# Layer norm's 1e-5 on GpSimd, a new order of all operations, and another turn of the w2 buffers (gated long convolution and token mixer, one core)

## The chip, the core and the metric

The kernel runs on one core of a Trainium2 chip. Five engines of that core work from queues of their own, each strictly in order: TensorE (PE in the profile, its weight loads PEld), VectorE (DVE), ScalarE (ACT), GpSimd (POOL) and SyncE (SP), which issues most DMAs. An instruction waits in its queue until the semaphores it needs have their values, and all behind it on that engine wait with it. The metric is the device time of one execution in microseconds, as a median of several runs.

## The reference, cut to what matters

```python
x = A_q                                            # 1 x 2048 x 640, bfloat16
g = sigmoid((x * gate_w).sum(-1, keepdims=True))
# a: a long convolution
k_shift = sum over t of k_pad[:, t:t+S] * shift_k[:, 3-t]     # 4 taps
kv = k_shift * v
y  = irfft(rfft(kv, 4096) * rfft(ssm_k, 4096))[:2048]         # along the sequence, per channel
a  = x * (y + kv * ssm_D)
# b: a token mixer
h = (x - mean) / sqrt(var + 1e-5)                  # layer norm over the 640 channels
u = gelu(einsum("bsd,sf->bdf", h, w1) + b1)        # w1: 2048 x 1536
b = transpose(einsum("bdf,fs->bds", u, w2) + b2)   # w2: 1536 x 2048
return g * a + (1 - g) * b
```

## The kernel before, in words

The sequence is cut into 16 tiles of 128 rows and four blocks of 512. **Branch a** is done as matrices: ssm_k is transposed on TensorE and brought into frequencies (stages wt and wf, `w_turn`, L1025, and `w_freq`, L1064, with the tables TFs, TFc and TS), joined and summed on VectorE (`w_comb`, L1098, `w_sums`, L1108). The blocks of k and v are loaded (`kv_load` and `kv_block`, L1124 to L1172): kT by a transposing DMA, four taps as small matmuls against the diagonal matrices dg, the result turned back by a second transposing DMA into kt, then products and sums on VectorE into v and es, and frequencies on TensorE (`a_freq`, stage af, L1174). `pair` (L1204) multiplies block spectra A with filter spectra W into Z on VectorE; `inverse` (L1272) brings Z back. **Branch b** is the layer norm (L915 to L945) with h for every tile, `mlp1` (stage m1, L961; h times w1, gelu to gT) and `mlp2` (stage m2, L1235; gT times w2). The `epilogue` (L1320) gates and adds, four tiles at a time; the last block goes tile by tile, the very last tile (`fin`) straight from PSUM in two halves.

**Layer norm.** Nine groups, two of one tile and seven of two. For each: `bn_stats` and `bn_aggr` on VectorE (L931, L933), then the addition of 1e-5 to the variance, vpe (L935; the instruction itself is in the helper `ts`, L664), then vpe to the power −0.5 on GpSimd, rstd (L936). Then, for tiles marked D, h on VectorE (L940, through L665); for the others a small product nmr on VectorE and h on ScalarE (L944, L945, through L695).

**w2.** `w2_load(q)` (L1228) brings 256 columns of w2 (768 KB, eight pieces) into one of three buffers, w2_0 to w2_2; `mlp2(q)` uses the same map. A load into a buffer waits for the last matmul that read it. In the profile all three show as `w<-in_B_w_dram`.

**What sets the order.** Every operation is first recorded with its engine (`_Plan.add`) and gets a number, 863 in all, in the order in which the program names it. `ORDER` (L433) is a hand-kept list of those 863 numbers; `_Plan.run` (L399) emits the operations in that order, so each engine's queue has its own operations in the order of the list, and gives matmul groups the free one of four PSUM slots that was used longest ago. `_Tracker` (L18) sets the semaphore waits. The planner's `cost` of an operation is kept with it but isn't used when a list is replayed.

Helpers that give most lines of the profile: matmuls L311; `tt` L657; `ts` L664 and L665; copies L672; fills L675; `act` L695; gathers L726; scatters L732; plain DMAs L262 and L265, transposing ones L260. SP's queue has all plain and transposing DMAs; GpSimd's has the gathers of reversed rows of v (`kv_load`), the scatters, and the DMAs that add into the output.

Of the kernel before, what the change touches and what calls it, by code (L numbers as in the profile page):

```python
# [12 lines left out]
ALU = mybir.AluOpType  # L13
# [409 lines left out]
def _checked(items, offs, base, top):  # L423
# [7 lines left out]


ORDER = [  # L433
# [36 lines left out]
]  # L470


def _build(nc, A_q, A_k, A_v, A_shift_k, A_ssm_k, A_ssm_D, B_x, B_w1, B_b1, B_w2, B_b2, gate_w, out):
# [19 lines left out]
    with ExitStack() as es:  # L493
# [146 lines left out]
        def bc(ap, dims):  # L640
            return bass.AP(tensor=ap.tensor, offset=ap.offset, ap=dims)
# [129 lines left out]
        def dram(t, off, ap):  # L771
            return bass.AP(tensor=t.tensor, offset=t.offset + off, ap=ap)

        b = bufs
# [107 lines left out]
        def rows(t, t0, cnt, w, c0, cw, step=1):  # L882
            return dram(t, t0 * 128 * w + c0, [[w, 128], [step * 128 * w, cnt], [1, cw]])
# [34 lines left out]
        for gi, (t0, cnt) in enumerate(groups):  # L918
            pr = 1.0 + t0 * 0.08
            plan.tag = f"ln{t0}"  # L920
            dma(x[:, t0:t0 + cnt, :], rows(A_q, t0, cnt, D, 0, D), f"x{gi}", pr)
            for t in range(t0, t0 + cnt):
                if LMODE[t] == "A":
                    act(h[:, t, :], x[:, t, :], ACT.Copy, pr, scale=-1.0 / (D * sq), acc=b["mv"][:, t, 0:1])
                    act(h[:, t, :], x[:, t, :], ACT.Square, pr, scale=1.0 / sq, bias=b["mv"][:, t, 0:1],
                        acc=b["mv"][:, t, 1:2])
                    continue
                for c in range(2):
                    o_ = b["stats"][:, t, c * 6:(c + 1) * 6]
                    i_ = x[:, t, c * HD:(c + 1) * HD]  # L930
                    vop("DVE", 0.393, (lambda o_, i_: lambda e: e.bn_stats(o_, i_))(o_, i_), [i_], [o_], pr, kind="bn")  # L931
                o_, i_ = b["mv"][:, t, :], b["stats"][:, t, :]
                vop("DVE", 0.11, (lambda o_, i_: lambda e: e.bn_aggr(o_, i_))(o_, i_), [i_], [o_], pr, kind="ba")  # L933
            sl = slice(t0, t0 + cnt)
            ts(b["vpe"][:, sl], b["mv"][:, sl, 1], 1e-5, None, ALU.add, None, pr, cost=0.07)  # L935
            vop("POOL", 0.7, (lambda o_, i_, e_: lambda e: e.tensor_tensor(o_, i_, e_, ALU.pow))(  # L936
                b["rstd"][:, sl], b["vpe"][:, sl], bc(c_mh, [[8, 128], [0, cnt]])), [b["vpe"][:, sl], c_mh], [b["rstd"][:, sl]], pr, kind="pow")
            for t in range(t0, t0 + cnt):
                if LMODE[t] == "D":
                    ts(h[:, t, :], x[:, t, :], b["mv"][:, t, 0:1], b["rstd"][:, t:t + 1],  # L940
                       ALU.subtract, ALU.mult, pr + 0.1, cost=0.36)
                else:
                    o_, a_, r_ = b["nmr"][:, t:t + 1], b["mv"][:, t, 0:1], b["rstd"][:, t:t + 1]
                    ts(o_, a_, r_, sq if LMODE[t] == "A" else -1.0, ALU.mult, ALU.mult, pr, cost=0.07)  # L944
                    act(h[:, t, :], x[:, t, :], ACT.Identity, pr, bias=o_, scale=r_)  # L945
# [280 lines left out]
                    tt(Z[:, 2, f0:f1, :], Z[:, 2, f0:f1, :], Z[:, 0, f0:f1, :], ALU.add, pr)  # L1226

        def w2_load(q):  # L1228
            nm = f"w2_{(0, 1, 0, 1, 2, 0, 1, 2)[q]}"
            dma(b[nm][:, :, :], dram(B_w2, q * 256, [[S, 128], [128 * S, FT], [1, 256]]), nm, 40.0 + q)  # L1230

        ost = []
# [2 lines left out]
        def mlp2(q):  # L1235
            plan.tag = f"m2_{q}"
            w2_load(q)
            w2 = b[f"w2_{(0, 1, 0, 1, 2, 0, 1, 2)[q]}"]
            o_ = b[f"o{(q // 2) % NO}"]
            turned = q >= 6  # L1240
            w2r = b[f"w2r{q % 2}"]
# [228 lines left out]
```

## Time and profile before

| | |
|---|---|
| median of 3 runs | 187.47 us (187.36 to 187.61) |
| profiled execution | 188.28 us |
| its span, first to last event | 186.4 us |
| granted TensorE clock | 1.00 |
| TensorE busy | 176.8 us |
| VectorE busy | 178.8 us |
| ScalarE busy | 127.1 us |
| GpSimd busy | 35.3 us |
| read from and written to HBM | 26.03 and 7.54 MB |

Times in the profile count from the start of the span. Busy time of an engine is the union of its instructions, which overlap where they are pipelined: a matmul of 0.30 us is followed by the next after about 0.14. A row of a timeline gives the start, the length of a run of like instructions, engine, line, output and inputs, and in brackets how long the engine sat idle before it and what it waited for. A row of a group gives the count, then after the bar the busy time in us, the mean of one in ns, and after the second bar the idle time ahead of them. DMA issues show on SPq.

### The profile page before, as it was taken

Reading aid. Unit: us, or ns where it says so; the run is one execution under the profiler, and the core shown is the slowest. Engines: PE = TensorE matmul, PEld = TensorE weight load, DVE = VectorE, ACT = ScalarE, POOL = GpSimd, SP = SyncE. Lnnn points to the kernel's source line nnn. Section 1 sums busy time; section 2 is a strip of 40 time slices with the busy share of each in tenths; the row PEclk is TensorE's granted clock in tenths of the full one; section 3 lists DMA queues with packets and bytes.
Section 4 is the critical chain, followed back from the end, with each engine's and each line's share of the span. In section 5 each row is a group of like instructions: output and inputs, shape, how many; then the busy total and the mean of one; then the engine's idle time right before and its main releaser. Section 6 shows DMA issues by size and latency. Waiting matters only on the chain.

```text
span 186.4 us, 3923 instructions
## 1 busy us (share of the span) xinstructions
PE 176.8 (95%) x1578; PEld 122.0 (65%) x1578; DVE 178.8 (96%) x252; ACT 127.1 (68%) x205; POOL 35.3 (19%) x68
## 2 busy tenths in 40 slices
PE   7778899999999999999999999999999999999992
PEld 2255667566667766777777777677776777777771
DVE  7999999999999999999899999999999999999784
ACT  3979899879499579638830146644889555875870
POOL 8367067610000000011000000000000500350262
PEclk9999999999999999999999999999999999999999
DMA  5999999798995998598769999988999998999394
GB/s 148 344 311 242 168 184 232 212 212 211 240 333 120 221 234 195 117 224 219 161 143 175 270 252 211 216 156 263 282 270 294 281 190 242 320 182 234 72 136 146
DMA packets 80448, 40.37 MB, mean 217 GB/s; under 512 B 39400, under 2 KB 80238, under 8 KB 80430
## 3 DMA queue, kind: packets, MB, share of 16 engines
q1 hardware_dynamic: 77694, 37.18, 80.9%
q0 software_dynamic: 2736, 2.95, 10.2%
q8 instruction: 12, 0.20, 0.5%
q14 instruction: 6, 0.05, 0.1%
HBM read 26.03 MB, written 7.54 MB: 180 GB/s over the span
## 4 chain that ended last, share of the span: by engine, by line
PE 64%; DVE 23%; DMA 6%; issue 2%; POOL 2%; ACT 1%; DVEq 0%; POOLq 0%
PE pp L311 64%; DVE stats L931 6%; DMA w<-in_B_w_dram 6%; DVE v L657 3%; DVE en L657 3%; DVE es L657 2%; DVE idx L664 2%; DVE W L657 2%; POOL rstd L936 1%; DVE h L665 1%; DVE eo L1023 1%; DVE mv L933 1%; DVE A L657 1%; DVE xe L657 1%; DVE dg L1012 1%
## 5 line engine op out<-in xcount | busy, mean ns | idle before, releaser
L311 PE MATMUL pp<-h,w 128*128 128x320 bf16 x384 | 56.6, 299 | 0.2
L311 PE MATMUL pp<-gT,w 128*128 128x320 bf16 x336 | 48.7, 299 | 0.6 <-DMA w<-in_B_w_dram 0.5
L311 PEld LDWEIGHTS pp<-h,w 128*128 128x128 bf16 x384 | 36.8, 98 | 15.9 <-issue 1.6
L311 PEld LDWEIGHTS pp<-gT,w 128*128 128x128 bf16 x336 | 32.5, 98 | 13.9 <-DMA w<-in_B_w_dram 1.1
L657 DVE TENSOR_TENSOR tt<-A,W 128x3840 bf16<-128x3840 bf16 (+2 forms) x16 | 27.8, 1738 | 0.2
L695 ACT ACTIVATE A<-pp 128x640 bf16<-128x640 f32 x32 | 21.3, 703 | 8.1 <-PE pp L311 8.1
L657 DVE TENSOR_TENSOR Z<-Z,tt 128x3840 bf16<-128x3840 bf16 (+1 forms) x14 | 26.1, 1867 | 0.1
L262 POOL DMA_DIRECT2D out_dram<-xe x3 | 4.1, 1367 | 66.4 <-DVE y L657 57.5
L695 ACT ACTIVATE pq<-pp 128x640 bf16<-128x640 f32 x16 | 11.0, 703 | 7.2 <-PE pp L311 7.1
L695 ACT ACTIVATE gT<-pp,bf 128x640 bf16<-128x640 f32 x12 | 9.5, 791 | 7.9 <-PE pp L311 7.9
L695 ACT ACTIVATE o<-pp,c,omg 128x640 bf16<-128x640 f32 x13 | 11.5, 881 | 4.6 <-PE pp L311 4.6
L931 DVE BATCH_NORM_STATS2 stats<-x 128x6 f32<-128x320 bf16 x32 | 13.7, 473 | 0.0
L695 ACT ACTIVATE xe<-xe,gg 128x640 bf16<-128x640 bf16 x16 | 12.8, 827 | 0.9 <-DMA xe<-rows_q 0.8
L695 ACT ACTIVATE ks<-pp 128x512 bf16<-128x512 f32 (+1 forms) x24 | 11.3, 523 | 3.1 <-PE pp L311 3.1
L657 DVE TENSOR_TENSOR Z<-A,W 128x3840 bf16<-128x3840 bf16 x6 | 12.8, 2153 | 0.5 <-PE pp L311 0.5
L695 ACT ACTIVATE W<-pp 128x640 bf16<-128x640 f32 x18 | 12.1, 720 | 1.5 <-PE pp L311 1.5
L675 POOL MEMSET W<- 1x640 bf16 x4 | 2.7, 665 | 51.1 <-ACT nq L695 49.8
L657 DVE TENSOR_TENSOR W<-W 128x2560 bf16<-128x2560 bf16 x8 | 11.9, 1486 | 0.2
L311 PE MATMUL pp<-kT,dg 64*64 64x256 bf16 x320 | 10.2, 270 | 0.3 <-ACT Wo L695 0.3
L657 DVE TENSOR_TENSOR Z<-Z 128x1280 bf16<-128x1280 bf16 (+1 forms) x16 | 10.0, 653 | 0.1
L311 PE MATMUL pp<-eo,TFc 128*128 128x320 bf16 x48 | 8.9, 300 | 1.2 <-ACT TFc L695 1.2
L262 POOL DMA_DIRECT2D out_dram<-rows_o x6 | 7.0, 1355 | 15.3 <-DMA out_dram<-o 13.2
(156 smaller groups left out, 305.1 us busy)
## 6 DMA issues: line engine op xcount, KB each, us to landing
w<-in_B_w_dram SPq DMA_DIRECT2D x24, 256.0 KB, 4.5
w<-in_B_w_dram SPq DMA_DIRECT2D x8, 768.0 KB, 6.2
wnat<-in_A_ssm_k_dram SPq DMA_DIRECT2D x4, 640.0 KB, 5.2
x<-in_A_q_dram SPq DMA_DIRECT2D x7, 320.0 KB, 6.5
out_dram<-o SPq DMA_DIRECT2D x6, 320.0 KB, 5.4
v<-in_A_v_dram SPq DMA_DIRECT2D x4, 320.0 KB, 3.9
rows_q<-in_A_q_dram SPq DMA_DIRECT2D x8, 160.0 KB, 3.5
xe<-rows_q SPq DMA_DIRECT2D x8, 160.0 KB, 6.1
```

The costliest lines, as they stand in the source:

```text
L262: ins = engobj.dma_start(out_ap, in_ap, accum_op=ALU.add)
L311: ins = self.nc.tensor.matmul(ps_ap, lhsT=lhsT, rhs=rhs, start=start, stop=stop)
L657: return vop(eng, c, lambda e: e.tensor_tensor(out_, in0, in1, op), [in0, in1], [out_], pr, kind="tt")
L664: return e.tensor_scalar(out_, in0, s1, None, op0=op0)
L665: return e.tensor_scalar(out_, in0, s1, s2, op0=op0, op1=op1)
L675: return vop(eng, 0.03 + nel(ap) / 1200.0, lambda e: e.memset(ap, val), [], [ap], pr, kind="ms")
L695: return e.activation(out_, src, func, **kw)
L931: vop("DVE", 0.393, (lambda o_, i_: lambda e: e.bn_stats(o_, i_))(o_, i_), [i_], [o_], pr, kind="bn")
L933: vop("DVE", 0.11, (lambda o_, i_: lambda e: e.bn_aggr(o_, i_))(o_, i_), [i_], [o_], pr, kind="ba")
L936: vop("POOL", 0.7, (lambda o_, i_, e_: lambda e: e.tensor_tensor(o_, i_, e_, ALU.pow))(b["rstd"][:, sl], b["vpe"][:, sl], bc(c_mh, [[8, 12 ...
L1012: vop("DVE", 1.45, lambda e: e.tensor_tensor(o_, ib, sb, ALU.mult), [i_, s_ap], [o_], 1.8, kind="tt")
L1023: vop("DVE", 0.74, lambda e: e.tensor_copy(dst, src()), [src], [dst], 0.3, ps=[p_], kind="ev")
```

## The change

Three edits.

1. The addition of 1e-5 (nine of them, the vpe operations) goes from VectorE to GpSimd, with another planner cost.
2. `ORDER` is another list of the same 863 numbers. Its first operations keep their places up to the exchange of a neighbour here and there; from about the 48th on, nearly every place differs. On GpSimd an addition stands ahead of its power, mostly right ahead; the powers no longer stand together, and the first gather for v0 (number 291), which stood behind the fill of a TFs row (number 41), stands ahead of it. The products and sums of TensorE, VectorE and ScalarE are the same, and so are the DMAs.
3. The pieces of w2 go to buffers 0, 1, 0, 2, 1, 0, 2, 1 in place of 0, 1, 0, 1, 2, 0, 1, 2: pieces 3 and 6 to buffer 2, pieces 4 and 7 to buffer 1.

```diff
 ORDER = [
-    0, 3, 7, 10, 62, 1, 2, 5, 9, 8, 244, 13, 11, 243, 14, 31, 206, 12, 19, 137, 26, 4, 15, 21,
-    126, 6, 54, 27, 33, 22, 91, 32, 16, 23, 63, 153, 64, 20, 211, 24, 287, 65, 17, 209, 103, 34, 25, 37,
...
-    825, 826, 832, 792, 831, 783, 793, 796, 781, 835, 780, 836, 797, 794, 803, 845, 855, 841, 784, 856, 804, 842, 857, 844,
-    840, 852, 805, 782, 853, 846, 798, 806, 799, 854, 800, 858, 860, 801, 861, 802, 859, 847, 862, 848, 850, 849, 851,
+    0, 3, 7, 10, 62, 1, 2, 5, 9, 8, 244, 13, 11, 243, 14, 31, 12, 206, 19, 137, 26, 4, 15, 21,
+    126, 6, 54, 27, 33, 91, 22, 32, 16, 23, 153, 63, 64, 20, 211, 24, 287, 65, 17, 209, 103, 34, 25, 66,
...
+    829, 834, 791, 833, 792, 781, 835, 783, 836, 797, 780, 803, 844, 841, 856, 845, 793, 840, 782, 842, 804, 843, 846, 805,
+    860, 794, 784, 847, 861, 798, 855, 806, 862, 852, 799, 853, 800, 857, 801, 854, 858, 802, 848, 859, 850, 849, 851,
 ]
...
             sl = slice(t0, t0 + cnt)
-            ts(b["vpe"][:, sl], b["mv"][:, sl, 1], 1e-5, None, ALU.add, None, pr, cost=0.07)
+            ts(b["vpe"][:, sl], b["mv"][:, sl, 1], 1e-5, None, ALU.add, None, pr, eng="POOL", cost=0.25)
             vop("POOL", 0.7, (lambda o_, i_, e_: lambda e: e.tensor_tensor(o_, i_, e_, ALU.pow))(
...
         def w2_load(q):
-            nm = f"w2_{(0, 1, 0, 1, 2, 0, 1, 2)[q]}"
+            nm = f"w2_{(0, 1, 0, 2, 1, 0, 2, 1)[q]}"
...
-            w2 = b[f"w2_{(0, 1, 0, 1, 2, 0, 1, 2)[q]}"]
+            w2 = b[f"w2_{(0, 1, 0, 2, 1, 0, 2, 1)[q]}"]
```

Numbers that matter at the end: 848 and 850 are the two halves of the last tile on VectorE, 860 and 861 additions of o, 847 the operation that adds the bias c2 to the last tile; 798 to 802 are TensorE's last groups. At the start of the w1 matmuls 163 is TensorE's first; 197 is a group of w1 matmuls that stands as the 75th operation of TensorE in both lists.

64 rows, old and new, of the table ORDER are left out of this document.

## The prediction

> **What bounds the kernel now.** I read the page's busy line first, then the chain of work that ended last, then the busy time in stretches.
>
> ```profile
> PE 176.8 (95%) x1578; PEld 122.0 (65%) x1578; DVE 178.8 (96%) x252; ACT 127.1 (68%) x205; POOL 35.3 (19%) x68
> PE 64%; DVE 23%; DMA 6%; issue 2%; POOL 2%; ACT 1%; DVEq 0%; POOLq 0%
> 49.76 67.37 PE pp L311 x644
> 117.26 15.95 PE pp L311 x151
> 133.21 10.31 DMA w<-in_B_w_dram
> 143.57 36.61 PE pp L311 x268
> 180.20 0.89 ACT o L695
> 183.14 0.55 DVE xe L1358
> 8.00:20.00 12.00, 9.46 (x86) 6.19 (x86) 12.00 (x39) 10.44 (x19) 6.58 (x8) 1.00 1.15 282
> 20.00:35.00 15.00, 14.54 (x228) 9.94 (x225) 14.90 (x50) 14.18 (x27) 8.46 (x11) 1.00 0.93 177
> 35.00:51.00 16.00, 15.41 (x112) 10.02 (x109) 15.97 (x24) 12.01 (x19) 1.80 (x3) 1.00 0.96 236
> 51.00:117.00 66.00, 66.00 (x637) 47.24 (x634) 65.14 (x54) 41.06 (x69) 1.24 (x2) 1.00 0.88 206
> 117.00:144.00 27.00, 26.42 (x227) 18.92 (x227) 26.79 (x22) 18.80 (x35) 0.00 (x0) 1.00 1.01 245
> 144.00:180.00 36.00, 36.00 (x268) 25.80 (x266) 34.58 (x46) 24.57 (x32) 9.43 (x9) 1.00 0.92 214
> ```
>
> Each row of the last block is a stretch, its length, then busy time of PE, PEld, DVE, ACT and POOL, the granted clock, the DMA share and GB/s. Two engines are full at once. To about 50 us the chain runs through VectorE, from there through TensorE, broken by one load and by the end. TensorE's idle time by these rows is 12.00 − 9.46 = 2.54, then 0.46, 0.59, 0, 0.58 and 0 us. So whatever the change does, it can gain only in the start-up, at the w2 load at 133.21 and behind TensorE's last matmul; and a late VectorE costs at once, since it has no slack before 144.
>
> The profiled execution took 188.28 us with a span of 186.4, so 1.9 lie around the span; the median of the runs shown is 187.47. I work out differences within the span and take them off the median.
>
> **The 1e-5 on GpSimd.** Nine additions leave VectorE and join GpSimd's queue.
>
> ```profile
> L664 DVE TENSOR_SCALAR vpe<-mv 128x2 f32<-128x2 f32 x7 | 1.1, 158 | 0.0
> L664 DVE TENSOR_SCALAR vpe<-mv 128x1 f32<-128x1 f32 x2 | 0.3, 147 | 0.0
> 23.42 0.17 DVE L664 TENSOR_SCALAR vpe<-mv 128x2 f32<-128x2 f32 x1
> 23.50 0.20 DVE L933 BATCH_NORM_AGGREGATE mv<-stats 128x2 f32<-128x12 f32 x1
> 24.85 5.34 POOL L936 TENSOR_TENSOR rstd<-vpe,cst 128x2 f32<-128x2 f32 x7 [6.87 <-DVE vpe L664]
> L936 POOL TENSOR_TENSOR rstd<-vpe,cst x9: 563/704/1073, 10.8 to 29.3; 128x2 f32<-128x2 f32 x7, 128x1 f32<-128x1 f32 x2
> L672 POOL CAST hcol<-hcol_i 128x2 f32<-128x2 int32 x1 | 0.4, 355 | 0.0
> L664 POOL TENSOR_SCALAR idp<-id_i 128x128 bf16<-128x128 int32 x1 | 0.9, 857 | 0.0
> L675 POOL MEMSET cst<- 128x1 f32 x7 | 0.4, 108 | 0.3 <-POOLq L1455 0.3
> ```
>
> The busy time removed is 1.1 + 0.3 = 1.4 us, but the next instruction starts 23.50 − 23.42 = 0.08 after an addition, so what VectorE gets back is nearer nine times 0.06 to 0.08, some 0.6 us, and only where nothing else waits. The trace has no such addition on GpSimd. Its bounds are a fill of 108 ns and a 128x128 operation of 857 ns; I take 0.35 us, from the row nearest in shape (128x2 float32, 355 ns). Nine cost 3.2 us, beside the 6.87 us in which GpSimd sat waiting for an addition, so by itself this costs nothing. In exchange the seven powers, which ran in one heap from 24.85 to 30.19, come in the order in which their statistics end; each starts as soon as its group is done. The tightest is that of tiles 10 and 11: laid out, its power ends at about 30.0, and VectorE's nmr behind it comes at 30.2. With 0.35 it fits by 0.1 to 0.25; at 0.857 it is 0.5 late, and behind that nmr stand all of VectorE's operations (the h tiles, then the W and kv products), so VectorE would lose 0.5. At 0.108 nothing is gained beyond.
>
> The powers themselves aren't steady: 563 to 1073 ns, median 704 (the three figures of their row), and the long ones are those beside VectorE's h operations behind 27.5. The Trainium skill, page "SBUF — State Buffer", section "Who interferes with whom", says that VectorE in its two-port modes, or with two SBUF inputs against a GpSimd reader, and GpSimd lock one port pair for a whole instruction and block each other fully. By that rule each new addition could wait for a whole h of VectorE, and the third rival below would come true; the long powers agree with it, but this trace has no addition there.
>
> **The start-up in the new order.** The first ops stay; then wf1's chain is moved ahead of wf0's, and on GpSimd the gather of v0 goes ahead of a fill that TensorE needs.
>
> ```profile
> 12.77 2.51 POOL L726 DMA_INDIRECT v<-in_A_v_dram,rev  x1 [0.20 <-issue]
> 15.29 0.20 POOL L675 MEMSET TFs<- 1x128 bf16 x1
> 12.05 0.99 PE L311 MATMUL pp<-eo,TFc 128*128 128x320 bf16 x6 [1.18 <-ACT TFc L695]
> 18.45 0.73 PE L311 MATMUL pp<-idp,en 128*128 128x128 bf16 x10 [0.52 <-DVE eo L1023]
> 16.75 0.95 ACT L695 ACTIVATE h<-x,nmr,rstd 128x640 bf16<-128x640 bf16 x1
> PE pp L311 <- DVE v L657: 0.3, 1, 0.3
> 24.63 3.20 SPq L260 DMA_TRANSPOSE kt<-ks  x1
> ```
>
> I laid TensorE's new queue end to end, each op with its own duration from the trace and held back to its producers. The old waits of 1.18 at 12.05 and 0.52 at 18.45 are filled with other work. But the fill of the TFs row now stands behind an addition, a power and the gather: about 12.8 + 2.51 + 0.2 puts it at 15.3 to 15.5, where TensorE wants it at about 14.4: 0.95 lost. The ScalarE h operation of 0.95 that now goes ahead of an evacuation costs TensorE some 0.9. TensorE then starts the first w1 matmuls 1.0 behind, and the SP queue's first kt transposition (24.63 before, 3.20 long) goes out about 0.7 later, with the v0 load behind it, which VectorE needs just when it lands. What brings it back: between 35 and 51 TensorE was idle 0.59, and more by starts, since the last of these waits (0.3 for v) ends at VectorE, which is 0.6 to 0.85 earlier by its removed additions. The layout brings TensorE to operation 197 (74 operations stand ahead of it in both lists, of the same durations) at 51.2 against 51.4: **−0.2**. That 1 us is lost and won back makes this the least certain term; the bounds are −0.5 and +1.6, the latter if none of the late start is recovered but its first part.
>
> **w2 buffers and the long middle.** Load q3 took the place of q1 in buffer 1, so it waited for q1's last matmul. It now goes to buffer 2, which nothing used before.
>
> ```profile
> 116.70 0.43 PE L311 MATMUL pp<-v,AFc 128*128 128x320 bf16 x2
> 142.81 0.30 PE L311 MATMUL pp<-gT,w 128*128 128x320 bf16 x1
> 143.57 0.72 PE L311 MATMUL pp<-gT,w 128*128 128x320 bf16 x4 [0.46 <-DMA w<-in_B_w_dram]
> 131.44 4.57 SPq L265 DMA_DIRECT2D w<-in_B_w_dram  x2
> w<-in_B_w_dram SPq DMA_DIRECT2D x2, 768.0 KB, 10.1
> ```
>
> Two matmuls of 0.30 take 0.43 together, so the next one starts some 0.14 behind; TensorE would have gone on at 142.81 + 0.14 = 142.95 instead of 143.57: 0.62. The same count at the first w2 piece (the row at 117.26 in the chain) is 117.26 − 116.70 − 0.28 = 0.28; its load stands earlier in SP's new list. Together **−0.90** at most. The new load has no buffer to wait for, but it isn't short: the two that went out from 131.44 took 10.1 us to land, one of them with no wait for a buffer. With the issue at about 130.7 it lands at 140.5 to 141, and TensorE, earlier by then, wants it at 140.4 to 141. Piece q4 then waits for buffer 1 instead, but it is wanted 6 us after q3 (48 matmuls of 0.14), so that wait is covered.
>
> What is late next: VectorE and ScalarE deliver to TensorE with 0.05 to 0.5 us of margin at ten places between 51 and 144, since all three run nearly full. Where TensorE gets ahead by 1 us these waits come up. Three I can name: the second v2 load behind its transposition on SP (0.4), the last products of a pair on VectorE into a matmul of its inverse (0.2) and the w2 pieces themselves (0.1 to 0.7). I take **+0.7** of new waits, bounds 0.3 and 1.6.
>
> **The end.** The new VectorE list puts the two last additions of o and the scaling of the last tile ahead of work that waits for TensorE.
>
> ```profile
> 180.00 2.88 PE L311 MATMUL pp<-gT,w 128*128 128x320 bf16 x20
> 181.53 0.48 DVE L657 TENSOR_TENSOR xe<-xe,pq 128x640 bf16<-128x640 bf16 x1
> 182.45 0.57 DVE L664 TENSOR_SCALAR xe<-xe,c 128x640 bf16<-128x640 bf16 x1
> 183.14 1.01 DVE L1358 SCALAR_TENSOR_TENSOR xe<-pp,omg,xe 128x320 bf16<-128x320 f32 x2
> 182.56 2.00 SPq L265 DMA_DIRECT2D out_dram<-xe  x3
> ```
>
> TensorE's last matmul ends at 182.88; the second of VectorE's two last operations ends at 183.14 + 1.01 = 184.15, 1.27 later, because the two stand behind 181.53 to 182.9. With those done before, the first half runs while TensorE does the second, and only one operation of 0.5 and its start follow: 0.65. **−0.62**, and nothing new stands in its way: TensorE's last six ops have the same order. From VectorE's end to the end of the span nothing changes (2.3 us, the write to DRAM). Bounds: 0 if an o of ScalarE comes as late as before against TensorE, −0.7 at most.
>
> **Sum.** −0.2 − 0.90 + 0.7 − 0.62 = −1.0 us, so a span of 185.4 and a median of 187.47 − 1.0 = 186.4.
>
> **Rivals.** First, the other side: **the start-up costs more than it gets back.** Place: the TFs fill behind the gather, then kt and v0 on SP. Price: 0.95 + 0.9, and up to 1.6 still there at 51. It decides from about 1.0 us: then 1.0 + 0.7 − 0.90 − 0.62 = +0.2. At 1.6 the sum is +0.8, 188.2; if new waits in the middle come to their upper bound too, 189. For it: VectorE, full to 174, has no place to catch up but its 0.6. Against: the end and the w2 wait don't depend on it.
>
> Second, **the w2 map doesn't do what it says**: the load takes 10 us by itself, and TensorE waits at q3 as before. Then −1.0 + 0.62 = −0.4: 187.1. For it, the 10.1 us without a wait; against, the issue is 2.5 us sooner.
>
> Third, **GpSimd is late with the powers**: additions of 0.7 to 0.86 us put nmr and all VectorE behind it back by 0.5: −0.5, 187.0. For it, the powers of up to 1.07; against, 6.87 us of idle GpSimd ahead.
>
> Fourth, gains and new waits cancel within 0.2%: between two full engines with margins of tenths this needs no single cause.
>
> **How the numbers follow.** A measurement of this kernel can tell about 0.2% (0.4 us) from no change. Chances: forecast (185.3 to 186.9) 0.42; w2 load late 0.10; GpSimd late 0.10; cancelled 0.13; start-up lost 0.25. The first three are faster by over 0.2%: 0.62. The range goes from the sum with the lower bound of each term (−0.5 − 0.90 + 0.3 − 0.7 = −1.8, and up to 0.4 more if VectorE gets back half of what lies between 0.6 and the 1.4 us of busy time: 185.3) to 188.4, just past the first rival's 188.2, which leaves some 0.1 of it above. The likeliest case alone has 185.3 to 186.9.
>
> **What would show it.** Nine TENSOR_SCALAR rows vpe on POOL: about 0.35 each right, above 0.7 the third rival. The powers spread from 17 to 30, the last nmr not waiting for one. A TensorE wait for a POOL fill near 15 of about 1 us; operation 197 at 51.2 right, at 52.5 the first rival. No wait for a w load at q3. A last VectorE operation 0.65 behind TensorE's last, not 1.27. I am wrong if TensorE's idle time from 51 to 180 grows beyond 0.58 + 0.7, or if one of the loads on SP, moved behind a transposition, lands after VectorE wants it.

## The result, and the profile after

The changed kernel took 191.06 us in the median of six runs (188.76 to 193.53), the kernel before 187.67 (187.36 to 188.03); the ratio is 1.0119 with a 95% interval of 1.0077 to 1.0161. On another chip the two stood at 191.12 (twelve runs) and 188.01, ratio 1.0079 (1.0036 to 1.0121). It is slower, by 0.8 to 1.2% in the ratio, where some 0.6% faster was forecast. The ratios leave out runs more than 1.5% above a kernel's fastest; since the changed kernel scatters over 5 us, its medians lie further up than its ratios. The medians are 3.39 us apart and the two profiled executions (188.28 and 190.51) only 2.23, so the traces below show two thirds of the loss.

The page of the changed kernel, first its busy line and its chain by engine, then the pieces of the chain that answer to those of before:

```profile
PE 177.3 (94%) x1578; PEld 122.7 (65%) x1578; DVE 178.2 (94%) x243; ACT 126.9 (67%) x205; POOL 40.0 (21%) x77
PE 71%; ACT 10%; DMA 9%; DVE 6%; issue 1%; POOL 1%; DVEq 0%; POOLq 0%; ACTq 0%
34.77 0.62 POOL W L675
35.56 9.75 DMA v<-in_A_v_dram,rev
45.43 1.56 DVE v L657 x2
50.87 54.92 PE pp L311 x456
113.83 57.96 PE pp L311 x522
185.89 0.55 DVE xe L1358
```

VectorE lost its place in the start of the chain: 23% before, 6% now. ScalarE has 10% and a load has come in at 35.56 that wasn't there. The long TensorE run starts at about the same place, but its end is later. The same stretches as before (length, busy time of PE, PEld, DVE, ACT, POOL, granted clock, DMA share, GB/s):

```profile
8.00:20.00 12.00, 9.27 (x69) 6.13 (x70) 12.00 (x41) 9.73 (x18) 6.19 (x14) 0.86 1.13 298
20.00:35.00 15.00, 14.21 (x231) 10.06 (x232) 14.65 (x38) 14.81 (x28) 6.22 (x13) 1.00 0.69 165
35.00:51.00 16.00, 14.00 (x101) 9.70 (x102) 13.92 (x21) 10.90 (x18) 8.90 (x6) 1.00 0.95 227
51.00:117.00 66.00, 65.81 (x604) 45.82 (x603) 64.82 (x54) 39.76 (x67) 1.24 (x2) 1.00 0.86 195
117.00:144.00 27.00, 27.00 (x257) 19.47 (x256) 26.12 (x21) 16.46 (x31) 0.00 (x0) 1.00 1.04 241
```

Two things stand out. The clock column, 1.00 everywhere before, is 0.86 from 8 to 20. And from 35 to 51 TensorE is idle for 2.00 us (0.59 before) and VectorE for 2.08 (0.03 before). At 117 to 144, where the w2 wait was, TensorE has no idle time left.

Where the 2.23 us of span went (186.45 to 188.68), counted in the two traces by the start of TensorE's operation 197 and the end of its last matmul:

| | before | after | difference |
|---|---|---|---|
| start to operation 197 | 51.39 | 53.86 | +2.47 |
| operation 197 to the end of the last matmul | 131.49 | 131.99 | +0.50 |
| end of the last matmul to the end of the span | 3.57 | 2.83 | −0.74 |

**The clock.** Stretches of the changed kernel and rows of TensorE's timeline, then the same places of the kernel before:

```profile
12.00:13.00 1.00, 1.00 (x6) 0.54 (x5) 1.00 (x3) 0.94 (x4) 0.80 (x2) 0.50 1.21 331
13.00:14.00 1.00, 1.00 (x5) 0.56 (x4) 1.00 (x4) 0.64 (x1) 0.99 (x3) 0.50 1.16 196
11.52:14.94 3.42, 3.29 (x13) 1.91 (x14) 3.42 (x12) 2.76 (x6) 2.97 (x7) 0.50 1.20 286
8.61 0.45 PE L311 MATMUL pp<-idp,en 128*128 128x128 bf16 x5 [2.35 <-DVE en L672]
11.65 1.25 PE L311 MATMUL pp<-eo,TFc 128*128 128x320 bf16 x4 [1.34 <-ACT eo L695]
12.69 2.34 PE L311 MATMUL pp<-eo,TFs 128*128 128x320 bf16 x8
18.52 0.70 PE L311 MATMUL pp<-eo,TFs 128*128 128x320 bf16 x4
```

```profile
12.00:13.00 1.00, 0.95 (x7) 0.70 (x8) 1.00 (x3) 0.60 (x1) 0.80 (x3) 1.00 1.08 348
13.00:14.00 1.00, 1.00 (x10) 0.72 (x8) 1.00 (x2) 0.38 (x1) 1.00 (x1) 1.00 1.90 149
8.24 1.74 PE L311 MATMUL pp<-idp,en 128*128 128x128 bf16 x20 [1.03 <-DVE en L657]
```

TensorE is busy all through 12 to 14, yet only five or six matmuls start in each microsecond, where seven and ten did before. Eight matmuls take 2.34 us; at full clock four of the same form take 0.70. The half clock lasts from 11.52 to 14.94, right after two idle times of 2.35 and 1.34 us; before they were 1.03 and 1.18, and the clock held. Not all of that is the order: the warm-up got full speed at 4.7 in this execution and at 6.6 in the one before, so it ended 1 us sooner. The order itself leaves TensorE 1.70 us of work between the two idle times (8.61 to 10.31), where it had 2.63 (8.24 to 10.87).

**The second gather of v1.** Three rows of GpSimd's timeline and one of VectorE's, then GpSimd's two rows of the kernel before:

```profile
34.77 0.62 POOL L675 MEMSET W<- 1x640 bf16 x1 [3.41 <-ACT nq L695]
35.56 5.97 POOL L726 DMA_INDIRECT v<-in_A_v_dram,rev  x1 [0.16 <-issue]
41.56 1.76 POOL L664 TENSOR_SCALAR flp<-fl_i 128x128 f32<-128x128 int32 x1
45.43 0.83 DVE L657 TENSOR_TENSOR v<-kt,v 128x1280 bf16<-128x1280 bf16 x1 [2.08 <-DMA v<-in_A_v_dram,rev]
```

```profile
12.03 0.54 POOL L664 TENSOR_SCALAR flp<-fl_i 128x128 f32<-128x128 int32 x1
17.03 0.95 POOL L726 DMA_INDIRECT v<-in_A_v_dram,rev  x1 [0.30 <-DVE stats L931]
```

Operation 328, the second gather of v1, went out at 17.03 before and had landed long before it was needed. The new list puts it behind the fill of the W row, which waits for ScalarE until 34.77. It then holds GpSimd for 5.97 us instead of about 1, lands at 45.31, and VectorE waits 2.08 for it; TensorE waits behind VectorE. The late start alone would not have done it. From its end on GpSimd the gather takes another 3.8 us to land, so with the 1.52 us that it takes in e3b_both (below) it would have landed at about 40.9 (an estimate from these rows), and VectorE asks for it at 43.35. It needed both, the wait of the fill and the 5.97 us.

### The profile page after: what moved, and what is told of

It is laid out like the page before. It is cut to its first block, busy times and chain, and to the rows that moved or that the text cites. A ratio compares the mean times of both kernels' runs of the same rounds, so it can differ in the third digit from the quotient of the medians.

```text
span 188.7 us, 3933 instructions
## 1 busy us (share of the span) xinstructions
PE 177.3 (94%) x1578; PEld 122.7 (65%) x1578; DVE 178.2 (94%) x243; ACT 126.9 (67%) x205; POOL 40.0 (21%) x77
## 4 chain that ended last, share of the span: by engine, by line
PE 71%; ACT 10%; DMA 9%; DVE 6%; issue 1%; POOL 1%; DVEq 0%; POOLq 0%; ACTq 0%
PE pp L311 71%; DMA v<-in_A_v_dram,rev 5%; DMA xt<-in_A_q_dram 4%; ACT ks L695 2%; ACT W L695 2%; ACT Wo L695 2%; ACT h L695 2%; DVE idx L664 2%; ACT eo L695 2%; DVE v L657 1%; DVE en L657 1%; DVE es L657 1%; DVE W L657 1%; ACT TFs L695 0%; ACT adx L695 0%
## 5 line engine op out<-in xcount | busy, mean ns | idle before, releaser
L311 PE MATMUL pp<-gT,w 128*128 128x320 bf16 x336 | 48.2, 299 | 0.0
L262 POOL DMA_DIRECT2D out_dram<-rows_o x6 | 6.4, 1260 | 17.1 <-DMA out_dram<-o 12.6
```

Source lines behind the costliest of these rows:

```text
L262: ins = engobj.dma_start(out_ap, in_ap, accum_op=ALU.add)
L311: ins = self.nc.tensor.matmul(ps_ap, lhsT=lhsT, rhs=rhs, start=start, stop=stop)
```

## The experiments

Theory A: the loss lies in the start-up, and it is the lower clock and the late gather. Theory B: the new order is slow throughout. Theory C: the additions on GpSimd are late. Each group of runs shared a chip with runs of the kernel before; ratios are to those. Operation 197 is read from one profiled execution of each kernel, the clock from all runs.

**First group (before 187.85).** The edits, in the changed kernel:

```diff
 ORDER, e1b_gather
-    ... 370, 155, 369, 336, 371, 162, 331, 171, 328, 337 ...
+    ... 370, 155, 369, 336, 328, 371, 162, 331, 171, 337 ...
 e2b_warm (863 is a new last operation, five matmuls on wz)
-    NWARM = 15
+    NWARM = 19
-    ... 144, 256, 92, 263, 145 ...
+    ... 144, 256, 92, 863, 263, 145 ...
 e4b_vpe_dve
-    ... pr, eng="POOL", cost=0.25)
+    ... pr, cost=0.07)
```

> The changed kernel with one exchange in its order: the second gather of v1 goes back ahead of the fill of the W row on GpSimd. Theory A (two losses in the start-up: the gather of v1 that went out at 35.56 and landed at 45.31, and the clock that fell to half from 11.2 to 14.8): VectorE's wait of 2.08 at 43.3 goes, TensorE's waits of 1.21 and 0.8 behind it too, the clock stays at 0.98 to 0.99; 1.5 to 2.1 us less than the changed kernel, about 189.2 with the same spread of some 4 us from run to run. Theory B (the new order is slow throughout, because VectorE and ScalarE deliver later): the wait only moves, 191. Theory C (the additions on GpSimd are late and hold up VectorE): 191.

> The changed kernel with matmuls on a constant tile that nothing reads: four more in the warm-up (19 for 15) and five in TensorE's wait ahead of wf1. They leave the computation as it is. Theory A: granted clock 1.000 in every run, the spread shrinks to about 0.5 us, and 1.5 to 1.7 us less than the changed kernel at clock 0.99 (3.3 us at half speed), more against the runs at 0.98: about 189.2. Theory B and C: the clock may rise, but TensorE then waits as long elsewhere: 191 in the median.

> Both edits at once: the gather of v1 ahead of the fill, and the nine matmuls that nothing reads. Theory A: both losses go, 3.3 to 3.8 us less than the changed kernel, 186.8 to 187.6, with the end 0.6 shorter than before. Theory B: at least 189.5. Theory C: 191.

> The changed kernel with the nine additions back on VectorE, at the same places of the list. Theory A: the cause isn't there; the same within the spread (190 to 191.5), clock 0.98 to 0.99, VectorE 0.6 fuller. Theory C: the additions' place on GpSimd is the cause: 188 or less, since the powers and what is behind them come on time.

| | median | ratio (interval) | granted clock below 0.995 | operation 197 |
|---|---|---|---|---|
| e1b_gather | 189.08 | 1.0049 (1.0017 to 1.0082) | 11 of 12 runs | 52.82 |
| e2b_warm | 188.88 | 1.0060 (1.0031 to 1.0090) | 2 of 12 | 53.91 |
| e3b_both | 187.45 | 0.9981 (0.9956 to 1.0005) | 2 of 12 | 51.25 |
| e4b_vpe_dve | 190.74 | 1.0141 (1.0084 to 1.0198) | 6 of 6 | 53.99 |

Theory C falls: with the additions back on VectorE nothing is won. A holds in both parts on this chip: with both mended the time is that of the kernel before, and taking back either edit alone costs time beyond the intervals (e1b_gather and e2b_warm against e3b_both). At operation 197 the two parts overlap. With the gather in time, the clock costs 52.82 − 51.25 = 1.57; that execution has two half-speed stretches (0.981), while the changed kernel's has one. With the gather late, mending the clock gains nothing there (53.91; 53.86 in the changed kernel). At full clock the gather costs 53.91 − 51.25 = 2.66. The medians with a late gather differ more (188.88 with the clock mended, 190.74 in e4b_vpe_dve, but their intervals overlap slightly), so what the clock is worth beside a late gather stays open. In e3b_both the gather takes 1.52 us and the waits of VectorE have no line for v; its stretches of the start-up:

```profile
8.00:20.00 12.00, 9.79 (x85) 6.58 (x86) 12.00 (x41) 10.61 (x20) 6.19 (x14) 1.00 1.15 293
35.00:51.00 16.00, 15.60 (x114) 10.58 (x112) 15.92 (x24) 11.96 (x19) 4.78 (x4) 1.00 0.98 227
```

**Second group (before 188.24): parts of the change in the old order.**

```diff
 f1_before_cold, kernel before
-    NWARM = 15
+    NWARM = 10
 f2_before_tail, kernel before: VectorE's last operations
-    845, 855, 856, 857, 844, 852, 853, 846, 858, 860, 861, 847, 848, 850
+    844, 856, 845, 846, 860, 847, 861, 855, 852, 853, 857, 858, 848, 850
 f3_before_map, kernel before: new w2 map, and in ORDER
-    ... 740 (load q4) ... 715 (load q3) ...
+    ... 715 ... 740 ...
 f4_both_oldmap, e3b_both: old w2 map, 715 moved behind 683
```

> The kernel before with its warm-up cut from 15 matmuls to 10, in the old order and with the old buffers. They write nothing that is read. Theory A (the granted clock follows TensorE's idle time in the start-up, not the new order as such): TensorE is idle for some 3 us ahead of 8.24, the clock falls as in the changed kernel, 0.98 to 0.99, and the time is 1.6 to 3.4 above the kernel before: 189.4 to 191.2, with a wide spread. Rival D (the clock is a matter of the chip or the execution): clock 1.000 and 187.8.

> The kernel before with the new order of VectorE's last 14 operations alone. If the end is worth what was forecast, VectorE's last operation ends 0.6 behind TensorE's last matmul instead of 1.27, and the time falls by 0.6: 187.2. Rival: ScalarE's o comes too late for it and nothing changes, 187.8.

> The kernel before with the new turn of the w2 buffers alone, the loads of q3 and q4 exchanged in SP's list so that q3, which now has a free buffer, goes first. If the wait of 0.62 at 143.57 is the buffer's: it goes, and since TensorE has work to the end, the time falls by 0.5 to 0.6: 187.2. Rival: the load takes 10 us by itself, so 0.2 at most is gained, or what is gained comes back as another wait: 187.6 to 187.9.

> The kernel with both edits (gather ahead of the fill, nine matmuls more) and the old turn of the w2 buffers, the load of q3 moved behind the last matmul that reads its buffer. If the map is worth 0.6 there: 0.5 to 0.6 more than with both edits, 188.0 to 188.1, with a TensorE wait for a w load. Rival: the new order hides that wait too, 187.5.

f1: 188.68, ratio 1.0042 (1.0010 to 1.0074); the clock fell in six of nine runs (0.978 to 0.991), so it does follow the idle time, in the old order too. But the time didn't rise as expected: the six runs at low clock have a median of 188.45, the three at full clock 189.86, and operation 197 stands at 51.37 as before. One reading is that in the old order VectorE sets the start-up and a slow TensorE hides behind it. Another is that the half-speed stretch of this execution, from 8.75 to 12.16, lies earlier and meets fewer matmuls. No run separates the two.

f2: 188.70, 1.0038 (1.0009 to 1.0067): the new tail by itself gains nothing. (The run also takes over the new places of a few of ScalarE's and GpSimd's last operations.) GpSimd's last rows, f2 first, then the kernel before:

```profile
181.41 1.10 POOL L732 DMA_INDIRECT out_dram<-xe,rev  x1 [1.85 <-DVE xe L657]
182.81 1.01 POOL L732 DMA_INDIRECT out_dram<-xe,rev  x1 [0.30 <-DVE xe L1358]
```

```profile
180.20 1.11 POOL L732 DMA_INDIRECT out_dram<-xe,rev  x1 [0.46 <-DVE xe L657]
181.89 1.01 POOL L732 DMA_INDIRECT out_dram<-xe,rev  x1 [0.59 <-DVE xe L657]
```

VectorE's last operation does end 0.84 behind TensorE's last matmul (182.96 and 182.12), not 1.27. But what was put behind for it are the additions that the two scatters wait for. They go out 0.9 to 1.2 later, and the chain of f2 ends with a scatter.

f3: 189.20, 1.0079 (1.0050 to 1.0108), slower, six of six runs. TensorE still waits for w2, and its row says at what:

```profile
143.21 2.35 PE L311 MATMUL pp<-gT,w 128*128 128x320 bf16 x16 [0.62 <-DMA w<-in_B_w_dram]
```

The load of q3 landed at 140.41, but the load of q4, which now waits for the buffer, went out at 133.94 and landed at 143.17, and the old order uses q4 ahead of q3. The wait moved with the buffer. Its profile also has a late kT transposition (TensorE waits 1.4 for it at 30); why every run is 1 us slower stays open.

f4: 189.07, 1.0026 (0.9992 to 1.0060), clock low in four of twelve. It has a w wait of 0.3 and, new, TensorE's 1.1 for VectorE's Z. Against e3b_both, by the ratios, the old map costs 0.45%, but the intervals overlap, and the third group shows where its wait for Z comes from: not from the map.

**Third group (before 188.30): the pieces of e3b_both.** g3 has the gather and NWARM = 19, g4 the gather and operation 863. The profiled execution of g3 has one half-speed stretch, those of the other three none.

> The kernel with both edits again, as the base of the three beside it. Theory A: 0.2 to 0.6 below the kernel before in the median, clock 1.000.

> Both edits, and the nine additions back on VectorE at the same places of the list. If the additions' move is worth what was forecast where nothing else covers it: 0.3 to 0.7 above the base, TensorE at operation 197 that much later than 51.25. Rival: VectorE has slack there in this order, no difference to the base (within 0.3).

> The gather ahead of the fill and the four more warm-up matmuls, without the five in the wait ahead of wf1. If the first idle time (6.25 to 8.61) is what lowers the clock: clock 0.99 to 1.000 in nearly every run and the time of the base within 0.4. If the second (10.3 to 11.65) does it: clock 0.98 to 0.99 in most runs, 1 to 1.7 above the base.

> The gather ahead of the fill and the five matmuls in the wait ahead of wf1, without the four more in the warm-up. If the first idle time lowers the clock: 0.98 to 0.99 in most runs, 1 to 1.7 above the base. If the second does: clock 0.99 to 1.000 and the time of the base within 0.4. If only the two together do: both this and its neighbour lie at the base.

| | median | ratio (interval) | clock below 0.995 | operation 197 |
|---|---|---|---|---|
| g1_both_again | 189.21 | 1.0020 (0.9981 to 1.0059) | 2 of 12 | 51.49 |
| g2_both_vpe_dve | 188.42 | 1.0032 (0.9994 to 1.0070) | 2 of 12 | 51.66 |
| g3_gather_nwarm | 189.08 | 1.0049 (1.0013 to 1.0085) | 11 of 12 | 52.40 |
| g4_gather_fill | 189.07 | 1.0032 (0.9995 to 1.0070) | 8 of 12 | 51.59 |

By the clock, both idle times count: either one filled alone leaves most runs at 0.99 (a single half-speed stretch), both filled leave two of twelve. One stretch costs 0.91 at operation 197 in g3 (52.40 against 51.49 in g1), where two cost 1.57 in e1b_gather; g4's 51.59 is from one of its four runs at full clock and says nothing of the price. By the time, g1 did not repeat e3b_both: on this chip it is not faster than the kernel before. Its VectorE timeline, then the same place in e3b_both:

```profile
131.52 2.15 DVE L657 TENSOR_TENSOR tt<-A,W 128x3840 bf16<-128x3840 bf16 x1
135.13 0.82 DVE L657 TENSOR_TENSOR v<-kt,v 128x1280 bf16<-128x1280 bf16 x1 [1.46 <-DMA v<-rows_v]
```

```profile
131.35 2.15 DVE L657 TENSOR_TENSOR tt<-A,W 128x3840 bf16<-128x3840 bf16 x1
133.45 0.83 DVE L657 TENSOR_TENSOR v<-kt,v 128x1280 bf16<-128x1280 bf16 x1
```

The last load of v3 landed at 133.43 in e3b_both, 0.02 us ahead of VectorE, and at 135.11 in g1. The new order has these loads (633 and 632 on SP) behind the w2 load of q2, which waits for a matmul. TensorE pays 0.9 for it at 170; in f4 VectorE has the same wait (1.7).

**Fourth group (before 188.01): the third part, and the clock alone.** h1 is the changed kernel; h3 and h4 have

```diff
-    ... 726, 631, ..., 705 (w2 load of q2), 633, 607, 632 ...
+    ... 726, 631, 633, 632, ..., 705, 607 ...
```

> The changed kernel itself once more, beside the three below. By theory A with its third part (see the next): 2.5 to 3.5 above the kernel before, clock 0.98 to 0.99 in every run.

> Both edits (gather ahead of the fill, nine matmuls more) as the base of the next. Between 0.2% below and 0.5% above the kernel before, as in its two earlier runs, with a spread of 3 us where the loads of v3 land after 133.5.

> Both edits, and on SP the last two loads of v3 back ahead of the w2 load of q2, as before the change. Theory A with a third part (in the new order these two loads stand behind the w2 load that waits for a matmul; where they land after 133.5 VectorE waits 1.5 and TensorE 0.9 at 170): 0.5 to 1.5 below the base where the base is disturbed, no VectorE wait for rows_v, and 0.2 to 1.0 below the kernel before. Rival (the spread of the base comes from other transfers): the same as the base.

> The gather and the loads of v3 mended, without the nine matmuls: only the clock is left of the three losses. Theory A: clock 0.98 to 0.99 in nearly every run and 1.0 to 1.7 above the kernel with all three edits. Rival (the clock's half speed is covered by VectorE, as it was in the old order with a short warm-up): within 0.4 of it.

h1: 191.12, 1.0079 (1.0036 to 1.0121), clock low in ten of twelve. Its profiled execution has the late gather (6.28 us) but full speed came to its warm-up at 6.7, its idle times were 1.36 and 1.34, and its half-speed stretch is from 20.37 to 23.78. So the two idle times make the low clock likely, and do not fix when it comes. h2: 189.11, 1.0018 (0.9979 to 1.0056). h3: 188.59, 1.0025 (0.9994 to 1.0056): no better than h2 by the ratio, so the expected gain of the third part didn't come. VectorE's wait for rows_v is gone, but TensorE's waits have a new line:

```profile
PE pp L311 <- DMA w<-in_B_w_dram: 2.3, 1, 2.3
```

The w2 load of q2 went out at the same time as in h2 (127.75 and 127.67) and landed at 136.02 instead of 132.85. From 126 to 136 the DMA share is 0.96 in h2 and 0.99 in h3, so the transfers compete there, and it looks as if who goes first makes the other late. That is argued from one execution of each: h3's took 189.87, well above its median, and h2's 187.57, well below its own. h4, without the nine matmuls: 189.81, 1.0090 (1.0059 to 1.0120), every run at 0.98 to 0.99, 1.2 above h3 in the median, with intervals that don't meet. With the gather in time the clock costs what A said.

**Fifth group (before 188.63): the old start-up with the new order behind it.** The first 362 places of the old list, the rest in the new list's order, new w2 map; i1 with the additions on VectorE, i2 on GpSimd.

> The first 362 places of the old list (to TensorE's operation 197 and one behind it), then all the rest in the new order, with the new turn of the w2 buffers and the additions on VectorE. Theory A (the loss is in the start-up, the new order from 51 on is as good or better): clock 1.000, TensorE at operation 197 at 51.4, no gather late; 187.2 to 188.4 as the kernel with both edits, 0.4 below to 0.4 above the kernel before, 2.5 to 3.5 below the changed kernel. Theory B (the new order is slow throughout): 189.5 or more.

> The same with the nine additions on GpSimd, at the places where the old list has them. If the addition's move by itself is worth what was forecast: 0.2 to 0.6 below its neighbour. Rival: the powers, still in one heap, come later by the additions ahead of them, and nothing is gained or 0.3 to 0.5 is lost.

i1: 190.69, 1.0132 (1.0086 to 1.0178). Theory A in its second half, that the rest of the new order is as good by itself, is not borne out, and the time is in the range of theory B: clock 1.00, operation 197 at 51.37, no w wait, but TensorE loses 2.2 us between 53 and 70 on en and A, which the two lists bring in different order. The halves of the lists don't fit each other, so the run says nothing of the new middle in its own surroundings.

i2: 192.17, 1.0188 (1.0152 to 1.0224), 1.5 above i1. Its powers stand in the old heap, now with an addition in front of each; VectorE's and TensorE's waits show it:

```profile
30.43 0.21 DVE L665 TENSOR_SCALAR nmr<-mv,rstd 128x1 f32<-128x1 f32 x1 [0.90 <-POOL rstd L936]
PE pp L311 <- DVE h L665: 1.9, 1, 1.9
```

## Why the prediction was wrong, point by point

**The bounds** held: nothing was won outside the start-up, TensorE's waits at 117 to 144 and the end. The range did not follow from them. The prediction itself gets 189 where the start-up and the middle both come to their upper bound, and ends its range at 188.4.

**The addition.** The GpSimd instruction takes 241 ns in the mean of the seven (0.35 taken), the powers spread over 11 to 30 as laid out, and the last nmr does not wait. But the 0.6 us for VectorE came to nothing that a pair of kernels shows: g1 and g2 differ by 0.17 at operation 197, the changed kernel and e4b_vpe_dve by 0.13. The third rival, late powers, is real, but only with the old heap (i2): there it costs 1.5, not 0.5.

**The start-up** is the step that failed: −0.2 was forecast (bounds −0.5 and +1.6), +2.47 was measured. Wrong was what the layout left out. It took every matmul at full clock, although the new order leaves TensorE less work between its first two waits, and the clock then fell to half. And of GpSimd's order it named one gather and passed over the other, 328, which the new list puts behind a fill that waits for ScalarE; the gather went out at 35.56, took 5.97 us and made VectorE wait 2.08. With both mended, one execution of e3b_both comes out at the forecast figures: operation 197 at 51.25 (51.2 forecast), a span of 185.4. Part of that is luck, since a cost of the layout did not occur: the TFs fill was not late, because the gather of v0 ahead of it took 1.23 us instead of 2.51. (The row shown for this fill, at 15.29, is number 42, which stood behind that gather before too; number 41, at 13.77 in the changed kernel, makes nobody wait.) The cost of ScalarE's h did occur: 0.9 forecast, a TensorE wait of 0.79 at 20.01. The first rival named the right place and side, with a price of 1.6 at 51 and another mechanism.

**The w2 buffers** did what was forecast: no wait of TensorE for a w load in the changed kernel. But one of the two waits in the −0.90 was misread, the 0.28 at 117.26:

```profile
109.95 0.37 SPq L265 DMA_DIRECT2D w<-in_B_w_dram  x1
w<-in_B_w_dram SPq DMA_DIRECT2D x1, 768.0 KB, 6.1
```

This load of the first w2 piece had landed at 116.03, 1.2 us earlier; in the trace the matmul waits for ScalarE's A, done at 117.11. The waits for w2 before were 0.62 at 143.57 and 0.15 at 133.16. f3 shows that the gain belongs to the new order, which uses q3 ahead of q4; the map alone only moves the wait.

**New waits in the middle**: +0.7 forecast; +0.50 in all with 1.05 of old waits gone (0.62, 0.15 and 0.28) makes about +1.5, near the bound of 1.6. They are many small ones (0.29 and 0.23 ahead of the gate matmuls, 0.19 at 171.82). The margin that was called thin for the v2 load decided at v3, by the chip: 0.02 us in e3b_both.

**The end**: −0.62 forecast, −0.74 measured; VectorE ends 0.59 behind TensorE (0.65 forecast). In f2 it is worth nothing, since there the scatters end last; the forecast's "nothing new stands in its way" is true of the new order and not of the edit by itself.

Both of A's parts are shown by pairs on one chip that differ in one of them: the clock by e1b_gather against e3b_both and h4 against h3, the gather by e2b_warm against e3b_both. Why the gather is slow there is argued below and not shown. Why f3 is slower in every run, and what besides the v3 loads spreads the kernels with both edits over 3 us on some chips, stays open. No version here beats the kernel before beyond its interval.

## What to carry to other kernels

When an order changes, list each moved instruction together with the wait of the one that now stands ahead of it, loads that go out early above all: a gather that costs 1 us of GpSimd put TensorE 2.7 us back at 51 because a fill ahead of it waited for ScalarE and it then ran at a place where it took 6 us. Idle time of TensorE in a start-up is not only lost time: in 16 of 18 runs of the changed kernel the clock fell to half for 3.4 us at a time, and with nine more matmuls to fill two of its waits in only two or three of 12. And an edit that is free or useful in one order (the w2 map, the tail, the addition) can cost 0.5 to 1.5 us in another; where two engines are full, price the pair, not the edit.

## What the runs showed of the hardware

**The clock** falls to exactly 0.50 for 3.41 us, or twice that, and comes back. In the changed kernel the warm-up matmuls start 0.43 us apart until 4.5 and 0.22 after it; the record of the granted clock begins with full speed at 4.70, and the low stretch runs from 11.52 to 14.94, two and three times 3.41 us later. In the kernel before the change from slow to fast came at 6.6. So the steps lie on a grid of 3.4 us whose start differs between executions, which fits the runs of one kernel at 1.000, 0.991 and 0.982 (none, one and two slow stretches). The Trainium skill, page "TensorE: Matmul & The Clock Gate", Part 1, describes a free-running window of 4096 cycles, about 3.4 us, in which activity is counted; the trace agrees with it in the length (3.41 us) and the moving start. What share of a window has to be busy, these runs don't settle. A window with TensorE busy 1.70 of 3.41 us (8.11 to 11.52 in the changed kernel) was followed by half speed, and so was one with 2.21 (16.95 to 20.37 in h1); windows with 1.55 (4.70 to 8.11 in the changed kernel) and 1.76 (5.34 to 8.76 in f2) were followed by full speed. Nor does the length of the idle times: i2, with the old start-up, had 2.29 and 1.18 in its profiled execution and kept full speed.

**A gather beside two-input VectorE operations** took four to six times as long. Operation 328 took 5.97, 6.73, 6.17 and 6.28 us in four kernels where VectorE ran TENSOR_TENSOR without a gap (35.5 to 41.4 in the changed kernel), and 0.95 to 1.52 elsewhere; right behind it in the changed kernel flp, which reads SBUF, took 1.76 for 0.54, while the fill ahead of it, which only writes, kept its 0.62. The page "SBUF — State Buffer" of the Trainium skill, section "Who interferes with whom", says that a VectorE instruction with two SBUF inputs contends with a GpSimd one that reads SBUF, and not with one that only writes. The rows of flp and of the fill agree with it in the changed kernel; whether a gather counts as such a reader, no run here shows. The prediction weighed that rule for the additions, where it did little (241 ns), and not for the gather. Where the gather goes out earlier, flp stands at that place instead, and it is the slow one, as in e3b_both:

```profile
33.68 0.62 POOL L675 MEMSET W<- 1x640 bf16 x1 [0.86 <-ACT nq L695]
34.28 4.21 POOL L664 TENSOR_SCALAR flp<-fl_i 128x128 f32<-128x128 int32 x1
```

In nine of the ten kernels with the early gather flp took 3.2 to 5.8 us there, and 0.57 in the tenth, g3, beside much the same VectorE operations, which that rule doesn't explain. So the slowness goes with the place and not with the gather alone. No run moved the VectorE operations away, so the cause is argued and not shown.
